# Attention of batches 2 to 7 gathered into four visits per batch of up to seven PSUM banks, with the next batch's projections joined to the last visit

## The chip, the cores and the metric

The kernel runs on one core of a Trainium2 chip. The metric is the device time of one execution in microseconds (us), the median of several runs.

## The reference

Linformer attention, then a feed-forward block with hard-swish, in float32. The kernel's matmuls take bfloat16 operands.

```python
# q, k, v: [8 batches, 8 heads, 1024, 64];  E, F: [64, 1024]
k_proj = einsum('ks,bhsd->bhkd', E, k)
v_proj = einsum('ks,bhsd->bhkd', F, v)
attn = softmax(q @ k_proj^T / 8)                 # over 64 projected positions
x = (attn @ v_proj)  -> [8192 tokens, 512]
# w_in: [512, 2048];  w_out: [2048, 512]
h = x @ w_in
out = (h * clip(h + 3, 0, 6) / 6) @ w_out
```

## The kernel before

Each batch is worked on in two halves `t` of 512 tokens. A half needs 16 **w_in groups** (4 full-array matmuls each, then a Relu on ScalarE and a product on VectorE) and 4 **w_out groups** (16 full-array matmuls each, then a copy and a store). The w_out groups of one half are done between the w_in groups of the next. Attention of batch b+1 is slipped into these groups of batch b, as a generator that is advanced one step after each group.

Attention of one batch has these parts. The matmuls of scores, sums and values use a quarter of the array each (64 rows x 64 columns, a **quadrant**), four side by side, a **round**. Those of the projection use 128 rows x 64 columns, two side by side. Such a way of splitting the array is called a **mode** here:

```python
def project(self):                 # 16 matmuls, each 128 rows x 64 columns of the array, one bank
    ps = self.ps = pat()
    for so in range(SO):
        for e in range(2):
            nc.tensor.matmul(ps[e * KP:(e + 1) * KP], ef_t[e][:, so, :], ...)

def scores(self, j):               # 8 quadrant matmuls, two banks, emptied by two Exp on ScalarE
    ...
def normalised(self, j):           # 8 quadrant matmuls, four banks
    den = self.quads(lambda r, h: ones[r:r + KP, :D], j)      # sums: two banks
    av = self.quads(lambda r, h: self.vp[r:r + KP, h, :], j)  # values: two banks
    lns = [log(den[t]) for t in range(NB)]                    # ScalarE
    yield
    for t in range(NB):                                       # 1/x = exp(-ln x) on ScalarE
        nc.vector.tensor_mul(self.xT[:, j, t, :], av[t], inverse(lns[t]))
        yield
```

The order in time is a plan of (steps to wait, part). Batches are counted from 0, as the code does. Batch 0 is done by a class of its own, batches 1 and 2 have plans of their own, and batches 3 to 7 use this one:

```python
PLAN = ((0, "project"), (1, "keys_out"), (0, "values_out", 0), (0, "values_out", 1), (1, "turn"),
        (6, "two_scores", 0), (3, "normalised", 0), (1, "normalised", 1),
        (1, "two_scores", 2), (3, "normalised", 2), (1, "normalised", 3))
PLANS = {1: (...), 2: (...)}
```

That makes seven places per batch where attention interrupts the stream of full-array matmuls, called **visits** here. PSUM, which the matmuls write to, is split into four banks for the feed-forward (`pmm`, "mm") and four for attention (`pat`, "at"):

```python
ps_mm = ctx.enter_context(tc.tile_pool(name="ps_mm", bufs=4, space=bass.MemoryType.PSUM))
ps_at = ctx.enter_context(tc.tile_pool(name="ps_at", bufs=4, space=bass.MemoryType.PSUM))
```

The softmax here doesn't subtract the row's maximum and nothing guards it: scores larger than these inputs give would overflow.

## Time and profile before

| | before |
|---|---|
| time, median of 4 runs | 518.1 us |
| span of the profiled run | 516.5 us |
| TensorE busy | 502.4 us, 97% |
| ScalarE, VectorE busy | 282.0 us, 239.4 us |
| one batch in the steady part (projection to projection) | 61.24 us |

The profile shows one execution. Its page has busy times by engine and the chain of waits that ended last. Its timeline lists instructions in order of time: start, duration from the first start to the last end, engine, source line, operation, output and inputs, shape, count, and in brackets the idle time ahead and what ended it. The ends of matmuls are modelled, so "busy" overlaps and hides gaps. Starts are what to trust: the steady step from one full matmul to the next is 0.216 us. About one full matmul in forty has no record (2048 are issued and 1998 recorded), so a lone jump of 0.216 us, often printed as "0.16 <-issue", is a lost record and no wait. The lines are shown inside the prediction.

### The profile page before, as it was taken

What the parts mean: (1) busy time and instruction counts of PE and PEld (TensorE: products, weight loads), DVE (VectorE), ACT (ScalarE), POOL (GpSimd) and SP (SyncE); (2) the same over time, 40 slices, a digit from 0 to 9 for tenths busy, and PEclk for the clock granted to TensorE, in tenths of its full rate; (3) what the DMA queues carried; (4) which work ended last, traced back from release to release, by engine and by line L of the source; (5) the groups of instructions that cost most, each with busy time, mean ns of one, the idle gap of its engine ahead of it and who ended that gap; (6) DMA issues with size and microseconds to landing.
All of it is one profiled execution on the core that took longest, in us unless ns stands there. A gap on an engine that the chain in (4) does not pass through costs nothing.

```text
span 516.5 us, 7173 instructions
## 1 busy us (share of the span) xinstructions
PE 502.4 (97%) x2752; PEld 222.7 (43%) x2802; DVE 239.4 (46%) x377; ACT 282.0 (55%) x517; POOL 37.2 (7%) x56
## 2 busy tenths in 40 slices
PE   8899999999999999999999999999999999999996
PEld 4444444434344444444444444444444444444442
DVE  3573735744455345445444453544535544344420
ACT  3657466575556743766436753566545674444431
POOL 8510020020020000200010000200000000000000
PEclk9999999999999999999999999999999999999999
DMA  9999999499169511984119820397111011001112
GB/s 169 202 204 208 202 162 209 93 155 212 41 103 214 123 43 30 153 175 102 41 52 188 175 67 34 70 205 151 41 42 39 34 42 41 28 35 43 41 43 80
DMA packets 73683, 55.40 MB, mean 107 GB/s; under 512 B 35504, under 2 KB 65456, under 8 KB 73648
## 3 DMA queue, kind: packets, MB, share of 16 engines
q0 software_dynamic: 31424, 29.36, 36.0%
q1 hardware_dynamic: 42000, 25.17, 18.3%
q8 instruction: 22, 0.36, 0.3%
q10 hardware_dynamic: 224, 0.39, 0.3%
q14 instruction: 13, 0.11, 0.1%
HBM read 59.24 MB, written 16.78 MB: 147 GB/s over the span
## 4 chain that ended last, share of the span: by engine, by line
PE 89%; DMA 3%; ACT 2%; issue 2%; DVE 2%; POOL 1%; another core or an unknown queue 0%; DVEq 0%; ACTq 0%; POOLq 0%
PE mm L421 41%; PE mm L401 41%; PE at L224 3%; PE at L181 3%; DMA w_in_sb<-in_moe_w_in_dram 2%; PE at L210 1%; DMA k<-in_k_dram 1%; DVE g L407 1%; ACT ln L158 0%; ACT r L406 0%; POOL q L97 0%; ACT aT L215 0%; POOL k L101 0%; DVE xT L235 0%
## 5 line engine op out<-in xcount | busy, mean ns | idle before, releaser
L407 DVE SCALAR_TENSOR_TENSOR g<-r,mm 128x512 bf16<-128x512 f32 x256 | 173.2, 685 | 207.0 <-ACT r L406 206.7
L401 PE MATMUL mm<-xT,w_in_sb 128*128 128x512 bf16 x1001 | 232.5, 379 | 3.4 <-issue 1.7
L421 PE MATMUL mm<-w_out_sb,g 128*128 128x512 bf16 x997 | 229.4, 379 | 1.3 <-issue 0.2
L406 ACT ACTIVATE r<-mm 128x512 f32<-128x512 f32 x256 | 152.2, 602 | 67.3 <-PE mm L401 65.6
L401 PEld LDWEIGHTS <-w_in_sb 128*128 128x128 bf16 x1024 | 97.0, 98 | 125.5 <-issue 12.8
L421 PEld LDWEIGHTS <-g 128*128 128x128 bf16 x1024 | 98.9, 98 | 120.6 <-issue 3.8
L435 ACT COPY o_sb<-mm 128x512 f32<-128x512 f32 x59 | 34.3, 586 | 140.0 <-PE mm L421 134.9
L235 DVE TENSOR_TENSOR xT<-at,rec 128x512 bf16<-128x512 f32 x56 | 38.0, 684 | 24.8 <-ACT rec L163 24.8
L163 ACT ACTIVATE rec<-ln 128x512 f32<-128x512 f32 x60 | 37.5, 637 | 0.0
L158 ACT ACTIVATE ln<-at 128x512 f32<-128x512 f32 x60 | 33.0, 615 | 6.2 <-PE at L224 3.9
L215 ACT ACTIVATE aT<-at 128x512 bf16<-128x512 f32 x56 | 29.0, 610 | 2.0 <-PE at L210 2.0
L199 POOL COPY mark<-kT 1x1 bf16<-1x1 bf16 x5 | 0.9, 177 | 246.6 <-DMA kT<-kp 246.6
L224 PE MATMUL at<-aT,vp 64*64 64x512 bf16 x112 | 12.7, 378 | 1.3 <-ACT ln L158 0.8
L181 PE MATMUL at<-k,e_t 128*64 128x512 bf16 x56 | 13.4, 382 | 0.0
L181 PE MATMUL at<-v,f_t 128*64 128x512 bf16 x56 | 13.4, 382 | 0.0
L224 PE MATMUL at<-aT,ones 64*64 64x512 bf16 x112 | 11.5, 400 | 0.1
L210 PE MATMUL at<-qT,kT 64*64 64x256 bf16 x224 | 9.1, 275 | 1.0 <-DVE vp L190 0.9
L190 DVE CAST vp<-at 64x512 bf16<-64x512 f32 x14 | 9.7, 694 | 0.3
L187 DVE CAST kp<-at 64x512 bf16<-64x512 f32 x14 | 8.9, 676 | 1.1 <-PE at L181 1.1
L181 PEld LDWEIGHTS <-e_t 128*64 128x64 bf16 x56 | 5.6, 109 | 7.3 <-issue 3.0
L84 PE MATMUL mm<-ones 128*128 128x512 bf16 x18 | 7.0, 521 | 1.5 <-DVE ones L77 1.5
L224 PEld LDWEIGHTS <-ones 64*64 64x64 bf16 x112 | 3.2, 103 | 11.9 <-issue 11.9
(57 smaller groups left out, 109.0 us busy)
## 6 DMA issues: line engine op xcount, KB each, us to landing
out_dram<-o_sb SPq DMA_DIRECT2D x63, 256.0 KB, 2.0
k<-in_k_dram POOLq DMA_DIRECT2D x7, 1024.0 KB, 14.7
v<-in_v_dram POOLq DMA_DIRECT2D x7, 1024.0 KB, 20.1
q<-in_q_dram POOLq DMA_DIRECT2D x7, 1024.0 KB, 9.8
w_out_sb<-in_moe_w_out_dram POOLq DMA_DIRECT2D x4, 512.0 KB, 18.0
w_in_sb<-in_moe_w_in_dram POOLq DMA_DIRECT2D x3, 512.0 KB, 12.4
k<-in_k_dram POOLq DMA_DIRECT2D x4, 256.0 KB, 5.5
v<-in_v_dram POOLq DMA_DIRECT2D x4, 256.0 KB, 7.7
```

The lines of the kernel that those rows point to most:

```text
L158: nc.scalar.activation(ln, den, AF.Ln)
L163: nc.scalar.activation(rec, ln, AF.Exp, scale=-1.0)
L181: nc.tensor.matmul(ps[e * KP:(e + 1) * KP], ef_t[e][:, so, :], kqv[self.b]["kv"[e]][:, :, so, :], start=(so == 0), stop=(so == SO - 1))
L210: nc.tensor.matmul(tiles[r][t * KP:(t + 1) * KP, a * HT:(a + 1) * HT], self.kT[r * D:(r + 1) * D, 2 * j + a, :], qT[r * D:(r + 1) * D, j, ...
L215: nc.scalar.activation(self.aT[j][:, r].rearrange("p a n -> p (a n)"), tiles[r], AF.Exp, scale=scale)
L224: nc.tensor.matmul(tiles[t][c:c + D].rearrange("p (r n) -> p r n", r=2), stationary(r, 2 * j + a), self.aT[j][r:r + KP, :, a, :], start=Tr ...
L235: nc.vector.tensor_mul(self.xT[:, j, t, :], av[t], inverse(lns[t]))
L401: nc.tensor.matmul(h_ps, w_in_sb[:, ko, fo * P:(fo + 1) * P], xT[:, ko, t, :], start=(ko == 0), stop=(ko == KO - 1))
L406: nc.scalar.activation(r, h_ps, AF.Relu, bias=0.5, scale=1.0 / 6.0)
L407: nc.vector.scalar_tensor_tensor(g[:, fo, :], r, 1.0, h_ps, op0=ALU.min, op1=ALU.mult)
L421: nc.tensor.matmul(o_ps, g[:, fo, c * P:(c + 1) * P], w_out_sb[:, fo, :], start=(fo == 0), stop=(fo == FO - 1))
L435: (copy or nc.scalar.copy)(o_sb, o_ps)
```

## The change

Its intent is to interrupt the stream of full-array matmuls less often. Attention of batches 2 to 7 becomes four visits, each inside a w_out group (after 8 of its 16 matmuls) or, for the last, behind one. To have banks for this, a visit borrows two or three "mm" banks. The copies of these w_out groups move to VectorE. The projection of batch b+2 follows directly on the last visit of batch b+1. The core of the diff (cuts marked "..."):

```diff
-    for lo, n in ((0, 128), (128, 128), (256, 256), (512, 512), (1024, 512), (1536, 512)):
+    for lo, n in ((0, 128), (128, 128), (256, 256), (512, 256), (768, 256),
+                  (1024, 512), (1536, 512)):
         load_w_in(lo, n)
...
+        def visit(self, n, following, later):
+            if n == 0:
+                last = self.scores(2, pmm)
+                firsts = [self.scores(j, pat) for j in range(2)]
+                for j, tiles in zip((2, 0, 1), (last, *firsts)):
+                    self.exps(j, tiles)
+                return lambda: None
+            if n == 1:
+                den, av = self.sums(0, pmm, pmm), self.values(0, pat, pat)
+                last = self.scores(3, pat)
+                recs = self.inverses(den)
+                self.exps(3, last)
+                return lambda: self.scaled(0, av, recs)
+            if n == 2:
+                den, av = self.sums(1, pmm, pmm), self.values(1, pat, pat)
+                more = self.sums(2, pat, pat)
+                ...
+                return lambda: self.scaled(1, av, recs)
+            early = self.values(2, pmm, pmm)
+            den, av = self.sums(3, pmm, pat), self.values(3, pat, pat)
+            if following:
+                following.project()
+            self.scaled(2, early, self.recs)
+            recs = self.inverses(den)
+            if following:
+                following.keys_out()
+                later += [following.turn] + [lambda a=a: following.values_out(a) for a in range(2)]
+            return lambda: self.scaled(3, av, recs)
...
         def normalised(self, j):
-            ...
-            lns = [log(den[t]) for t in range(NB)]
+            den, av = self.sums(j, pat, pat), self.values(j, pat, pat)
+            recs = self.inverses(den)
             yield
-            for t in range(NB):
-                nc.vector.tensor_mul(self.xT[:, j, t, :], av[t], inverse(lns[t]))
-                yield
+            self.scaled(j, av, recs)
+            yield
+            yield
...                                           # batch 1 keeps seven visits; (3, ...2), (1, ...0) become
+            (1, "two_scores", 0), (2, "two_scores", 2), (2, "normalised", 0),
...                                           # in the loop over w_in groups
+                rows = second_group(*behind[0], fo // SB, nc.vector.tensor_copy)
+                if n < 3:
+                    next(rows)
+                    next(rows)                # 8 of the 16 w_out matmuls
+                    rest = second.visit(n, third, later)
+                    whole(rows)
+                else:
+                    whole(rows)
+                    rest = second.visit(n, third, later)
+                rest()
```

Batch 1's visits are in batch 0's feed-forward. Batch 2's are in the second half of batch 1's, because that is the first place with w_out groups. Those of batches 3 to 7 are in the first half of the batch before.

More of the change, by code (lines that the diff above doesn't have):

```diff
@@ L156, in log @@
     def log(den):
-        ln = att.tile([P, TOK], f32, tag="ln", name="ln")
+        ln = att.tile([P, TOK], f32, tag="rec", name="rec", bufs=4)
         nc.scalar.activation(ln, den, AF.Ln)
@@ L161, in inverse, with __init__ @@
     def inverse(ln):
-        rec = att.tile([P, TOK], f32, tag="rec", name="rec")
-        nc.scalar.activation(rec, ln, AF.Exp, scale=-1.0)
-        return rec
+        nc.scalar.activation(ln, ln, AF.Exp, scale=-1.0)
+        return ln
     class Attention:
-        def __init__(self, b, xT):
-            self.b, self.xT = b, xT
+        def __init__(self, b):
+            self.b = b
             self.kp = att.tile([KP, H, 2, D], bf16, tag="kp", name="kp")
@@ L200, in turn, with scores @@
                 load_kqv(self.b + 1, "qkv" if self.b > 1 else "kvq")
-        def scores(self, j):
+        def scores(self, j, alloc):
             qT = qT_dma[self.b]
-            self.aT[j] = att.tile([P, 2, 2, HT], bf16, tag="aT", name="aT", bufs=KO + 1)
-            tiles = [pat() for _ in range(2)]
+            tiles = [alloc() for _ in range(2)]
             for a in range(2):
@@ L213, in scores, with exps @@
                                          start=True, stop=True)
+            return tiles
+        def exps(self, j, tiles):
+            self.aT[j] = att.tile([P, 2, 2, HT], bf16, tag="aT", name="aT", bufs=KO + 1)
             for r in range(2):
@@ L216, in scores, with quads @@
                                      AF.Exp, scale=scale)
-        def quads(self, stationary, j):
-            tiles = [pat() for _ in range(NB)]
+        def quads(self, stationary, j, allocs):
+            tiles = [alloc() for alloc in allocs]
             for t in range(NB):
@@ L227, in quads, with sums, values, inverses @@
             return tiles
+        def sums(self, j, *allocs):
+            return self.quads(lambda r, h: ones[r:r + KP, :D], j, allocs)
+        def values(self, j, *allocs):
+            return self.quads(lambda r, h: self.vp[r:r + KP, h, :], j, allocs)
+        def inverses(self, den):
+            recs = [log(d) for d in den]
+            for rec in recs:
+                inverse(rec)
+            return recs
+        def scaled(self, j, av, recs):
+            for t in range(NB):
+                nc.vector.tensor_mul(self.xT[:, j, t, :], av[t], recs[t])
@@ new lines, in visit @@
+        def visit(self, n, following, later):
[15 more added lines that the diff above has]
+                recs = self.inverses(den)
+                self.recs = []
+                later += [lambda i=i: self.recs.append(log(more[i])) for i in range(NB)]
+                later += [lambda i=i: inverse(self.recs[i]) for i in range(NB)]
+                return lambda: self.scaled(1, av, recs)
[9 more added lines that the diff above has]
+            return lambda: self.scaled(3, av, recs)
@@ L229, in normalised, with two_scores @@
+        def two_scores(self, j):
+            tiles = [self.scores(i, pat) for i in (j, j + 1)]
+            for i in range(2):
+                self.exps(j + i, tiles[i])
         def normalised(self, j):
-            den = self.quads(lambda r, h: ones[r:r + KP, :D], j)
-            av = self.quads(lambda r, h: self.vp[r:r + KP, h, :], j)
-            lns = [log(den[t]) for t in range(NB)]
+            den, av = self.sums(j, pat, pat), self.values(j, pat, pat)
+            recs = self.inverses(den)
@@ L233, in normalised @@
             yield
-            for t in range(NB):
-                nc.vector.tensor_mul(self.xT[:, j, t, :], av[t], inverse(lns[t]))
-                yield
-        def two_scores(self, j):
-            self.scores(j)
-            self.scores(j + 1)
+            self.scaled(j, av, recs)
+            yield
+            yield
         def steps(self, plan):
@@ L247, in steps @@
                 yield from getattr(self, part)(*args) or ()
-    PLAN = ((0, "project"), (1, "keys_out"), (0, "values_out", 0), (0, "values_out", 1), (1, "turn"),
-            (6, "two_scores", 0), (3, "normalised", 0), (1, "normalised", 1),
-            (1, "two_scores", 2), (3, "normalised", 2), (1, "normalised", 3))
-    PLANS = {1: ((0, "project"), (0, "keys_out"), (1, "turn"), (0, "values_out", 0), (2, "values_out", 1),
-                 (1, "two_scores", 0), (3, "two_scores", 2), (1, "normalised", 0),
-                 (0, "normalised", 1), (0, "normalised", 2), (0, "normalised", 3)),
-             2: ((10, "project"), (0, "keys_out"), (1, "turn"), (2, "values_out", 0), (3, "values_out", 1),
-                 (1, "two_scores", 0), (2, "two_scores", 2), (3, "normalised", 0),
-                 (0, "normalised", 1), (1, "normalised", 2), (0, "normalised", 3))}
+    PLAN = ((0, "project"), (0, "keys_out"), (1, "turn"), (0, "values_out", 0), (2, "values_out", 1),
+            (1, "two_scores", 0), (2, "two_scores", 2), (2, "normalised", 0),
+            (0, "normalised", 1), (0, "normalised", 2), (0, "normalised", 3))
     class First:
@@ L470 @@
             first.queries(1, (0, 1) if fo == FO - 2 else (2, 3))
-    ahead = Attention(1, x_next).steps(PLANS[1])
+    ahead = Attention(1)
+    ahead.xT = x_next
+    ahead = ahead.steps(PLAN)
     rows = [second_group(0, 0, g[0], c) for c in range(SB)]
@@ L492 @@
     xT = x_next
-    behind = []
+    behind, later = [], []
+    second = Attention(2)
     for b in range(1, B):
-        ahead = iter(())
         if b + 1 < B:
-            x_next = x_tile()
-            ahead = Attention(b + 1, x_next).steps(PLANS.get(b + 1, PLAN))
+            x_next = second.xT = x_tile()
+        third = Attention(b + 2) if b + 2 < B else None
+        n = 0
         for t in range(NB):
-            if t == 1 and b + 2 < B:
-                qT_dma[b + 2] = q_transposed(b + 2)
+            if b == 1 and t == 1:
+                qT_dma[3] = q_transposed(3)
             g = g_tile()
@@ L506 @@
                 first_group(xT, t, g, fo)
-                next(ahead, None)
-                if behind and fo % SB == SB - 1:
-                    whole(second_group(*behind[0], fo // SB))
-                    next(ahead, None)
+                if later:
+                    later.pop(0)()
+                if b > 1 and t == 0 and fo == 5 and third:
+                    qT_dma[b + 2] = q_transposed(b + 2)
+                if b == 1 and t == 0 and fo == 10:
+                    second.project()
+                    second.keys_out()
+                    later += [second.turn, *(lambda a=a: second.values_out(a) for a in range(2))]
+                if not behind or fo % SB < SB - 1:
+                    continue
+                if b + 1 == B or n == 4:
+                    whole(second_group(*behind[0], fo // SB))
+                    continue
+                rows = second_group(*behind[0], fo // SB, nc.vector.tensor_copy)
[8 more added lines that the diff above has]
+                rest()
+                n += 1
             behind = [(b, t, g)]
-        whole(ahead)
-        xT = x_next
+        second, xT = third, x_next
     for c in range(SB):
```

## The prediction

It was written before any run of the changed kernel.

> **What bounds the kernel now.** I read the page first: engine shares, then the chain that ended last.
>
> ```profile
> PE 502.4 (97%) x2752; PEld 222.7 (43%) x2802; DVE 239.4 (46%) x377; ACT 282.0 (55%) x517; POOL 37.2 (7%) x56
> ...
> PE 89%; DMA 3%; ACT 2%; issue 2%; DVE 2%; POOL 1%; another core or an unknown queue 0%; DVEq 0%; ACTq 0%; POOLq 0%
> ```
>
> TensorE is on the chain nearly everywhere; VectorE and ScalarE have half their time free. So a saving must come from TensorE's own order: idle stretches, or work that runs slower than its neighbours. The 97% hides both, because matmul ends are modelled. I therefore went to the timeline of TensorE and compared start times (its x counts miss a record now and then, so a lone jump of 0.216 us is a lost record). A steady stretch:
>
> ```profile
> 214.64 1.89 PE L401 MATMUL mm<-xT,w_in_sb 128*128 128x512 bf16 x8
> 216.46 0.41 PE L224 MATMUL at<-aT,ones 64*64 64x512 bf16 x4
> 216.70 0.39 PE L224 MATMUL at<-aT,vp 64*64 64x512 bf16 x4
> 217.02 1.90 PE L401 MATMUL mm<-xT,w_in_sb 128*128 128x512 bf16 x8
> 218.76 3.62 PE L421 MATMUL mm<-w_out_sb,g 128*128 128x512 bf16 x15
> ```
>
> A whole w_out group of 16 lasts 3.45 us elsewhere in that view (242.18 to 245.64), so a full-array matmul takes 0.216. The 16 full ones from 214.64 to 218.76 account for 3.45 of 4.12 us; the attention visit between them costs 0.67. Its work is two rounds of four quadrant matmuls. A 512-column round takes 0.2125 (the projection's pairs follow each other at that step), so 0.425. The other **0.24 us is the price of one visit**, half at each edge: the visit starts 0.31 after the last full matmul, and the next full one starts 0.31 after its last round.
>
> Second, real stalls. Attention of batch 2, in the timeline of 84 to 140 us:
>
> ```profile
> 104.25 0.51 PE L210 MATMUL at<-qT,kT 64*64 64x256 bf16 x9
> 105.64 0.41 PE L210 MATMUL at<-qT,kT 64*64 64x256 bf16 x7 [0.88 <-DVE vp L190]
> 105.98 1.90 PE L401 MATMUL mm<-xT,w_in_sb 128*128 128x512 bf16 x8
> ...
> 130.19 0.40 PE L224 MATMUL at<-aT,vp 64*64 64x512 bf16 x2
> 131.44 0.40 PE L224 MATMUL at<-aT,vp 64*64 64x512 bf16 x2 [0.85 <-ACT ln L158]
> 131.78 1.90 PE L401 MATMUL mm<-xT,w_in_sb 128*128 128x512 bf16 x8
> ```
>
> The visit needs an attention bank that VectorE or ScalarE has not emptied. And one at the start, where w_in arrives late:
>
> ```profile
> 22.80 1.46 PE L401 MATMUL mm<-xT,w_in_sb 128*128 128x512 bf16 x6
> 24.60 1.25 PE L401 MATMUL mm<-xT,w_in_sb 128*128 128x512 bf16 x5 [0.35 <-DMA w_in_sb<-in_moe_w_in_dram]
> ```
>
> **What the Trainium skill says.** "TensorEngine Tiling (Array Packing)", Tiling Modes, Key Properties: "Changing tiling mode (not just tile) drains the TensorE". The trace agrees: 0.09 to 0.10 us over the normal step at every edge between 128x128 and 64x64, and between 128x128 and 128x64. It gives no figure; mine is the trace's. "TensorE: Matmul & The Clock Gate", Part 2, says that back-to-back matmuls hide the array's drain (215.7 ns at 512 columns); the trace has 216. "PSUM — Partial Sum Buffer", Specifications, gives eight banks: four "mm" and four "at" here, so a visit that wants seven must borrow from the feed-forward ring.
>
> **The change, part by part.**
>
> *Fewer visits.* The instruction order of both builds has the same 5606 TensorE rows. Before, each of batches 1 to 7 makes 7 visits (projection, two of scores, four of sums and values): 49. After: batch 1 still 7, batch 2's projection 1, batches 2 to 7 four each: 32. That is 17 fewer, at 0.24 (0.25 for a projection, 0.23 for scores): 4.0 us. But five projections are joined to a 64x64 visit and remain another mode (128x64), so one edge each stays: 5 x 0.12 = 0.6. Net **-3.4 us**, all on the path.
>
> *Stalls of batch 2.* An undisturbed visit lasts 0.56 from first to next full matmul (216.46 to 217.02). Those at 104.25, 123.62 and 129.92 last 1.73, 1.02 and 1.86: 2.9 too many. After, batch 2's visits come in the second half of batch 1, one per 6.9 us plus the visit, with mm banks in reserve, and its projection bank is emptied several groups before. **-2.9 us**.
>
> *Stalls of batch 1.* 73.18 and 83.77 last 1.38 (one lost record taken out) and 1.15: 1.4 too many. The second pair of scores comes one step earlier and both products now follow together, ahead of the output copy; the banks come free 0.6 to 0.9 earlier. **-1.4 us**.
>
> *w_in piece halved.* The pieces land at 22.0 and 24.56, 2.55 us for 512 columns; half of that lands at an estimated 23.3, before its use at 24.1. The next half, about 24.6, is needed at 25.8. **-0.5 us**.
>
> *New work on the other engines: none on the path, but one place.* About 24 output copies move from ScalarE (586 ns) to VectorE (685 ns): VectorE 239 to 256 us, still half idle. I walked a steady batch with steps between queued instructions of 0.48 us (ScalarE) and 0.60 (VectorE). After the visit of three scores, six exponentials hold ScalarE for 3.0 us, and the next Relu waits for none of it, since half a w_out group (1.73) and a w_in group (0.86) lie between. The semaphores in the build show that the group after next takes the bank of the first exponential, not that of the output still being copied. After the visit with the projection VectorE has the copy, two products, two key casts and two products before the first Relu product: done an estimated 3.3 us after the visit, needed at 3.45. Tight, but it fits.
>
> *The place.* Batch 2's last visit ends right where batch 2's own feed-forward begins. Its fourth matmul needs the last product, and VectorE casts the keys first. From before:
>
> ```profile
> 98.24 1.28 DVE L187 CAST kp<-at 64x512 bf16<-64x512 f32 x2 [0.56 <-PE at L181]
> ```
>
> The casts end at 99.52, 1.42 us after the projection's next full matmul (98.10). The first product follows at +0.60, 2.03; the matmul was due at 0.66. **+1.4 us**, once. For later batches a half batch of feed-forward lies between.
>
> Sum: 518.07 - 3.4 - 2.9 - 1.4 - 0.5 + 1.4 = 511.3. I put 0.2 on top for small misses: **511.5 us**, -1.3%.
>
> **Rivals.** (a) *Bank waits move into the big visits.* A seven-bank visit needs nearly all of PSUM; if each of the 24 met 0.2 us of wait, 4.8 us would be lost: 516. Against it: the banks' last readers are done 2 us or more ahead in my walk; for it: the margin of 0.15 after the projection visit. (b) *The loads of batch 4.* They are asked for at the start of batch 2's half and its projection comes at the end of it, some 33 us later; before, v landed 21.5 us after the first of the three was issued (147.3 to 168.8), and qT stood in the queue for 13 us under such loads (113.1 to 126.4), holding output stores. By this there are 5 us in hand; if not, 1 to 4 us once. (c) *The edges are not the cost*: if the 0.24 came from waiting weight loads and grew with the visit, nothing of the 3.4 would be saved: 515. Against: the scores' 16 small matmuls pay 0.23, the projection's 16 large ones 0.25. (d) *VectorE becomes the bound around the visits*: 50% on average speaks against it.
>
> **Range and chances.** If all gains hold and the 1.4 shrinks, 510; if batch 1's gain fails and the big visits lose 0.05 to 0.1 each, 514. Range 510.0 to 514.0. Faster by over 2% needs 507.7, 3.8 us that I see nowhere: 0.03. Slower by over 2% (528.4) would need a stall of half a microsecond at each visit and more: 0.01. Within 2%: 0.96.
>
> **What would show it.** Steady batches one projection to the next (61.24 us, 200.71 to 261.94) should come to about 60.65. Visits of 0.09 at each edge, whatever their length, confirm the price; the joined visit should show a third edge. No stall over 0.2 us between 84 and 135 us, none near 24. One stall of 1.4 us at the fourth w_in matmul of batch 2, released by VectorE's product. It is wrong if idle time before w_in or w_out groups after the visits appears, released by VectorE, or if the first visit of a batch waits for its transposed keys.

## The result

The changed kernel takes **511.89 us** (median of 4 runs, 511.63 to 512.01) against 518.1 us (518.07 to 518.32) before. The ratio is 0.9879, with a 95% interval from 0.9861 to 0.9896: faster by 1.2%, within 2%. (A ratio here is the mean time of one kernel's fast runs over that of the other's of the same rounds, so it isn't quite the ratio of the medians quoted.)

The page of the changed kernel, engine shares and chain:

```profile
PE 497.4 (98%) x2750; PEld 224.3 (44%) x2802; DVE 257.5 (50%) x401; ACT 274.5 (54%) x493; POOL 37.9 (7%) x57
...
PE 94%; DMA 3%; issue 1%; POOL 1%; DVE 0%; ACT 0%; DVEq 0%; POOLq 0%
```

ScalarE and VectorE, 2% each of the chain before, are at 0% now (rounded), which fits: by its waits from 20 us on, TensorE stands still for another compute engine once, at the new stall shown below. VectorE has 18 us more to do, ScalarE 7.5 us less, and neither is near its limit.

A joined visit of the steady part, in the timeline of TensorE:

```profile
226.32 0.41 PE L227 MATMUL mm<-aT,vp 64*64 64x512 bf16 x4
226.56 0.38 PE L227 MATMUL mm<-aT,ones 64*64 64x512 bf16 x2
226.57 0.38 PE L227 MATMUL at<-aT,ones 64*64 64x512 bf16 x2
226.78 0.39 PE L227 MATMUL at<-aT,vp 64*64 64x512 bf16 x4
227.09 0.40 PE L181 MATMUL at<-k,e_t 128*64 128x512 bf16 x1
...
228.63 0.38 PE L181 MATMUL at<-v,f_t 128*64 128x512 bf16 x1
228.94 3.41 PE L450 MATMUL mm<-xT,w_in_sb 128*128 128x512 bf16 x15
232.41 3.62 PE L470 MATMUL mm<-w_out_sb,g 128*128 128x512 bf16 x16
```

The step between starts is 0.21 to 0.24 within a mode. It is 0.31 from the quadrants to the projection (226.78 to 227.09) and again from the projection to the full array (228.63 to 228.94): the joined visit has three edges, not four. From 228.94 to 232.41 is 3.47 us, the plain duration of 16 matmuls, so the w_out group after it waits for nothing. One steady batch (projection to projection) is 60.62 us now, from 61.24.

Batch 2's visits, in the same view:

```profile
106.21 0.41 PE L209 MATMUL mm<-qT,kT 64*64 64x256 bf16 x8
106.45 0.61 PE L209 MATMUL at<-qT,kT 64*64 64x256 bf16 x16
106.99 1.90 PE L470 MATMUL mm<-w_out_sb,g 128*128 128x512 bf16 x7
...
121.78 0.41 PE L227 MATMUL mm<-aT,ones 64*64 64x512 bf16 x4
122.02 0.39 PE L227 MATMUL at<-aT,vp 64*64 64x512 bf16 x4
122.24 0.39 PE L227 MATMUL at<-aT,ones 64*64 64x512 bf16 x4
122.56 1.90 PE L470 MATMUL mm<-w_out_sb,g 128*128 128x512 bf16 x8
```

Six banks are filled in 0.78 us each time without an idle mark. The waits of 0.9 us that batch 2's visits had are gone.

And the new stall. TensorE first, then VectorE, in the timeline around batch 2's last visit:

```profile
133.92 0.82 PE L450 MATMUL mm<-xT,w_in_sb 128*128 128x512 bf16 x2
135.98 2.97 PE L450 MATMUL mm<-xT,w_in_sb 128*128 128x512 bf16 x13 [1.25 <-DVE xT L246]
```

```profile
134.05 1.28 DVE L187 CAST kp<-at 64x512 bf16<-64x512 f32 x2 [0.76 <-PE at L181]
135.26 1.27 DVE L246 TENSOR_TENSOR xT<-at,rec 128x512 bf16<-128x512 f32 x2
```

The fourth w_in matmul needs the first of the two products, and VectorE does both key casts ahead of it. By starts the matmul came 1.41 us late.

### The profile page after: what moved, and what is told of

Same layout as the page of the kernel before. It is cut to its first block, busy times and chain, and to the rows that moved or that the text cites. A ratio compares the mean times of both kernels' runs of the same rounds, so it can differ in the third digit from the quotient of the medians.

```text
span 510.0 us, 7106 instructions
## 1 busy us (share of the span) xinstructions
PE 497.4 (98%) x2750; PEld 224.3 (44%) x2802; DVE 257.5 (50%) x401; ACT 274.5 (54%) x493; POOL 37.9 (7%) x57
## 4 chain that ended last, share of the span: by engine, by line
PE 94%; DMA 3%; issue 1%; POOL 1%; DVE 0%; ACT 0%; DVEq 0%; POOLq 0%
PE mm L470 43%; PE mm L450 43%; PE at L181 3%; DMA w_in_sb<-in_moe_w_in_dram 2%; PE at L227 1%; PE mm L227 1%; DMA k<-in_k_dram 1%; PE at L209 1%; PE mm L209 0%; PE at L370 0%; POOL q L97 0%; DVE kp L187 0%; POOL k L101 0%; PE at L350 0%; DVE xT L246 0%
## 5 line engine op out<-in xcount | busy, mean ns | idle before, releaser
L450 PE MATMUL mm<-xT,w_in_sb 128*128 128x512 bf16 x1001 | 229.2, 379 | 3.1 <-DVE xT L246 1.2
L484 ACT COPY o_sb<-mm 128x512 f32<-128x512 f32 x35 | 20.3, 587 | 91.5 <-PE mm L470 91.5
L484 DVE COPY o_sb<-mm 128x512 f32<-128x512 f32 x28 | 19.3, 691 | 67.3 <-PE mm L470 64.2
L159 ACT ACTIVATE rec<-mm 128x512 f32<-128x512 f32 x34 | 19.0, 595 | 34.1 <-PE mm L227 17.6
L163 ACT ACTIVATE rec<-rec 128x512 f32<-128x512 f32 x60 | 35.6, 637 | 0.0
L246 DVE TENSOR_TENSOR xT<-at,rec 128x512 bf16<-128x512 f32 x44 | 28.1, 680 | 7.1 <-ACT rec L163 7.1
L218 ACT ACTIVATE aT<-at 128x512 bf16<-128x512 f32 x44 | 23.1, 613 | 0.9 <-PE at L209 0.9
L159 ACT ACTIVATE rec<-at 128x512 f32<-128x512 f32 x30 | 17.3, 598 | 6.0 <-PE at L227 3.7
L218 ACT ACTIVATE aT<-mm 128x512 bf16<-128x512 f32 x12 | 6.5, 594 | 8.9 <-PE mm L209 8.9
L227 PE MATMUL at<-aT,vp 64*64 64x512 bf16 x88 | 8.5, 376 | 0.0
```

The costliest lines, as they stand in the source:

```text
L159: nc.scalar.activation(ln, den, AF.Ln)
L163: nc.scalar.activation(ln, ln, AF.Exp, scale=-1.0)
L218: nc.scalar.activation(self.aT[j][:, r].rearrange("p a n -> p (a n)"), tiles[r], AF.Exp, scale=scale)
L227: nc.tensor.matmul(tiles[t][c:c + D].rearrange("p (r n) -> p r n", r=2), stationary(r, 2 * j + a), self.aT[j][r:r + KP, :, a, :], start=Tr ...
L246: nc.vector.tensor_mul(self.xT[:, j, t, :], av[t], recs[t])
L450: nc.tensor.matmul(h_ps, w_in_sb[:, ko, fo * P:(fo + 1) * P], xT[:, ko, t, :], start=(ko == 0), stop=(ko == KO - 1))
```

## The experiments

Eleven runs; all results were correct. "Now" is the changed kernel, 511.89 us. Each experiment was timed beside the kernel before. Differences of a few tenths between whole times are not read as effects of an edit: the changed kernel itself took 511.89 and 511.42 us, and its first w_in matmul started at 20.68 us in one profile, where it waited 0.73 us for its weights to land, and at 20.36 in the other (19.9 to 21.0 over all runs).

### Is it the change of the array's mode that costs? Four runs

Theory: each change between ways of splitting the array costs about 0.12 us, whatever lies between. Rivals: any interruption costs it; or attention's own data and waits do; or it grows with the visit; or joining a projection is free. The last batch has no attention, so extra visits of a known kind can be put there: one after each of its 32 w_in groups, with matmuls of ones into an attention bank that nothing reads.

```diff
                 first_group(xT, t, g, fo)
+                if b + 1 == B:
+                    extra()
...
+    def extra():                                  # d_full
+        ps = pat()
+        for _ in range(2):
+            nc.tensor.matmul(ps, ones[:, :P], ones, start=True, stop=True)
+    def extra():                                  # d_quad; d_long has range(4)
+        ps = [pat(), pat()]
+        for _ in range(2):
+            for r in range(2):
+                for c in range(2):
+                    nc.tensor.matmul(ps[r][c * D:(c + 1) * D], ones[r * D:(r + 1) * D, :D],
+                                     ones[r * D:(r + 1) * D], start=True, stop=True)
+                                                  # d_mixed: range(1), then
+        for c in range(2):
+            nc.tensor.matmul(ps[0][c * D:(c + 1) * D], ones[:, :D], ones, start=True, stop=True)
```

> Changed kernel with 32 extra interruptions in the last batch (which has no attention), one after each w_in group: two full-array 128x512 matmuls of ones into a free attention bank, never read; the result stays right. Theory (the price is for changing the array's mode, not for interrupting): 32 x 2 x 0.216 = +13.8 us on 511.9, so 525.7. Rival (any interruption of the stream costs 0.24): 533.4.

> The same 32 places with two rounds of four 64x64 quadrant matmuls instead, the same array time. Theory: 32 x (0.425 + 0.24) = +21.3 us, so 533.2, that is 7.5 us over the full-array twin. Rival (the 0.24 comes from attention's own weights, data or waits, which the extra visits do not have): 525.5.

> The same 32 places with four rounds of quadrant matmuls. Theory (a price per visit): 32 x (0.85 + 0.24) = +34.9 us, so 546.8. Rival (the price grows with the rounds, 0.12 each): 32 x (0.85 + 0.48), so 554.5.

> The same 32 places with one round of quadrant matmuls and then one pair of 128x64 matmuls. Theory (each edge between modes costs 0.12, three edges here): 32 x (0.425 + 0.36) = +25.1 us, so 537.0. Rival (only leaving and re-entering the full mode costs, a joined projection is free): 533.2.

| run | time, us | ratio to before | edges per visit | per visit, by whole times |
|---|---|---|---|---|
| d_full | 525.32 | 1.0141 | 0 | +0.42 over now; its own two matmuls take 0.43 |
| d_quad | 532.39 | 1.0277 | 2 | +0.22 over d_full (7.07 / 32) |
| d_long | 546.60 | 1.0553 | 2 | +0.44 over d_quad (14.21 / 32), its two more rounds take 0.43 |
| d_mixed | 536.48 | 1.0356 | 3 | +0.13 over d_quad (4.09 / 32) |

One visit in the timeline of TensorE, first d_full, then d_quad, then d_mixed:

```profile
455.73 0.59 PE L550 MATMUL at<-ones 128*128 128x512 bf16 x2
456.16 1.03 PE L450 MATMUL mm<-xT,w_in_sb 128*128 128x512 bf16 x4
457.02 0.59 PE L550 MATMUL at<-ones 128*128 128x512 bf16 x2
```

```profile
459.18 0.63 PE L552 MATMUL at<-ones 64*64 64x512 bf16 x8
459.74 1.04 PE L450 MATMUL mm<-xT,w_in_sb 128*128 128x512 bf16 x4
460.71 0.63 PE L552 MATMUL at<-ones 64*64 64x512 bf16 x8
```

```profile
458.83 0.41 PE L552 MATMUL at<-ones 64*64 64x512 bf16 x4
459.17 0.41 PE L555 MATMUL at<-ones 128*64 128x512 bf16 x2
459.51 1.04 PE L450 MATMUL mm<-xT,w_in_sb 128*128 128x512 bf16 x4
460.48 0.41 PE L552 MATMUL at<-ones 64*64 64x512 bf16 x4
```

In d_full two matmuls and four come round in 1.29 us, which is 6 x 0.216 and nothing else. In d_quad the same array time takes 1.53, so 0.24 more. In d_mixed it takes 1.65. All four rivals fall: an interruption in the full mode is free, ones that wait for nothing pay the same as attention does, doubling the visit doesn't raise the price, and a change from 64x64 to 128x64 is charged like any other. Since d_long also has twice as many small matmuls and weight loads per visit as d_quad, their number is not what costs.

The whole times of the table also carry the scatter of the start. From the end of batch 7's projection to the last matmul, by starts, it is 155.64 us now, 169.45 in d_full, 176.83 in d_quad, 190.64 in d_long and 180.69 in d_mixed. Per visit that is 0.43 for two full matmuls, **0.23 for the two edges**, 0.43 for two more rounds and **0.12 for the third edge**, close to the single lines.

What fills the time at an edge is not shown. Within a mode the trace has each weight load start one matmul ahead of its use. At an edge it starts with its own matmul (both at 216.46 in the kernel before, 0.31 after the last full one), and a load lasts about 0.10 us. An array that has to empty first and a load that cannot go ahead would look the same here.

### Is it the number of visits in the changed kernel?

```diff
             if n == 0:
                 last = self.scores(2, pmm)
-                firsts = [self.scores(j, pat) for j in range(2)]
+                next(rows)                        # four more w_out matmuls
+                firsts = [self.scores(0, pat)]
+                next(rows)
+                firsts.append(self.scores(1, pat))
...
                 den, av = self.sums(0, pmm, pmm), self.values(0, pat, pat)
+                next(rows)
                 last = self.scores(3, pat)
...                                           # in the loop: the first visit starts after 4 matmuls, not 8
                     next(rows)
-                    next(rows)
-                    rest = second.visit(n, third, later)
+                    if n > 0:
+                        next(rows)
+                    rest = second.visit(n, third, later, rows)
```

> Changed kernel with the first visit of each of batches 2 to 7 cut into three and the second into two, each piece four w_out matmuls after the one before: 18 more visits, nothing else. Theory: 18 x 0.235 = +4.2 us on 511.9, so 516.1. Rival (the gain came from bank waits removed, not from fewer visits): 511.9.

Measured: 515.84 us (ratio to before 0.9953), 3.95 us over now, 0.22 for each of the 18 visits added. A steady batch goes from 60.62 to 61.31 us, 0.23 for each of three. The first visit, now in three pieces, in the timeline of TensorE:

```profile
201.73 0.41 PE L209 MATMUL mm<-qT,kT 64*64 64x256 bf16 x8
202.30 0.81 PE L474 MATMUL mm<-w_out_sb,g 128*128 128x512 bf16 x3 [0.16 <-issue]
203.04 0.41 PE L209 MATMUL at<-qT,kT 64*64 64x256 bf16 x8
203.39 1.04 PE L474 MATMUL mm<-w_out_sb,g 128*128 128x512 bf16 x4
204.35 0.41 PE L209 MATMUL at<-qT,kT 64*64 64x256 bf16 x8
```

From 203.04 to 204.35 is 1.31 us: four full matmuls (0.86), two rounds of 256 columns (0.22) and 0.23 of edges. (The row with three matmuls has lost one record.) The same work in more pieces costs what the pieces' edges cost.

### Batch 1's order of steps and the halved w_in piece alone

```diff
# kernel before
-        (256, 256), (512, 512), (1024, 512), (1536, 512)
+        (256, 256), (512, 256), (768, 256), (1024, 512), (1536, 512)
...                       # batch 1 alone; "joined" is the changed kernel's normalised()
-                 (1, "two_scores", 0), (3, "two_scores", 2), (1, "normalised", 0),
-                 (0, "normalised", 1), (0, "normalised", 2), (0, "normalised", 3)),
+                 (1, "two_scores", 0), (2, "two_scores", 2), (2, "joined", 0),
+                 (0, "joined", 1), (0, "joined", 2), (0, "joined", 3)),
```

> Kernel before with the halved w_in piece and batch 1's new order of steps (second scores one step earlier, both products together) and nothing else. Theory: 1.4 us of bank waits at two visits of batch 1 and 0.5 us of the wait near 24 us go: 518.1 - 1.9 = 516.2. Rival (these waits return further on, in the loads or the transposes of batch 1): 518.

Measured: 516.36 us, 1.79 under its kernel before (518.15; ratio 0.9966). From batch 1's projection to batch 2's, the profile has 39.61 us instead of 41.03: 1.42 less. The timeline of TensorE at the start and at the last of batch 1's visits:

```profile
21.83 4.52 PE L412 MATMUL mm<-xT,w_in_sb 128*128 128x512 bf16 x20
...
83.01 0.41 PE L224 MATMUL at<-aT,ones 64*64 64x512 bf16 x4
83.25 0.39 PE L224 MATMUL at<-aT,vp 64*64 64x512 bf16 x4
83.57 1.90 PE L432 MATMUL mm<-w_out_sb,g 128*128 128x512 bf16 x8
```

The 20 matmuls run through the place at 24 us where the stream had broken off for w_in. The visit lasts 0.56 instead of 1.15. From the first w_in matmul to batch 1's projection it is 35.87 us instead of 36.39, 0.52 less; in this profile that first matmul came 0.58 later than before, which hides the gain at the projection itself. Neither wait comes back later.

### Batch 2's waits alone

```diff
# kernel before, batch 2 alone, visits where they were
-             2: ((10, "project"), (0, "keys_out"), (1, "turn"), (2, "values_out", 0), (3, "values_out", 1),
-                 (1, "two_scores", 0), (2, "two_scores", 2), (3, "normalised", 0),
-                 (0, "normalised", 1), (1, "normalised", 2), (0, "normalised", 3))}
+             2: ((10, "project"), (0, "keys_out"), (1, "turn"), (0, "values_out", 0), (1, "values_out", 1),
+                 (5, "two_scores", 0), (2, "two_scores", 2), (3, "joined", 0),
+                 (0, "joined", 1), (1, "joined", 2), (0, "joined", 3))}
```

> Kernel before with only batch 2's steps changed, visits as before: its values are cast out of the projection bank three and five steps earlier, the reciprocals follow their logarithms at once and both products come together. Theory (waits for undrained attention banks cost 2.9 us at three visits of batch 2): 518.1 - 2.9 = 515.2, with undisturbed visits of 0.56 us. Rival (they waited for the batch's loads and transposed queries, which the change only moved out of the way): 517.5 to 518.5.

Measured: 516.24 us, 1.92 under its kernel before (518.16; ratio 0.9965). From batch 2's projection to batch 3's it is 39.82 us instead of 41.67, 1.86 less. The rival falls, but 1.0 to 1.1 us of the 2.9 is still there. (By the plan the values are cast two and four steps earlier, not three and five.) In the timeline of TensorE, then of VectorE:

```profile
103.34 1.02 PE L412 MATMUL mm<-xT,w_in_sb 128*128 128x512 bf16 x4 [0.20 <-DVE g L418]
...
122.59 0.41 PE L224 MATMUL at<-aT,ones 64*64 64x512 bf16 x4
123.05 0.40 PE L224 MATMUL at<-aT,vp 64*64 64x512 bf16 x2
123.65 0.40 PE L224 MATMUL at<-aT,vp 64*64 64x512 bf16 x2 [0.19 <-DVE xT L245]
123.98 3.63 PE L432 MATMUL mm<-w_out_sb,g 128*128 128x512 bf16 x16
```

```profile
121.71 0.69 DVE L418 SCALAR_TENSOR_TENSOR g<-r,mm 128x512 bf16<-128x512 f32 x1 [3.36 <-ACT r L417]
122.31 1.28 DVE L245 TENSOR_TENSOR xT<-at,rec 128x512 bf16<-128x512 f32 x2
```

The early casts themselves held up a w_in group, at 103.34, by 0.14 us by starts (a record is lost just before it). The visit at 106.69 takes 0.66, so 0.10 too much. And the visit at 122.59 takes 1.39 instead of 0.56, more than the 1.02 it took in the kernel before. That makes 1.07 us, all that is left.

The visit at 122.59 waits for the products of the visit before it, which lies only 3.45 us of w_in groups back. ScalarE first does a copy, two logarithms and two reciprocals (118.58 to 121.19) and then the first Relu (to 121.68). The two products stand in VectorE's queue behind the w_in product that needs this Relu. They end at 123.00 and 123.60, and the two pairs of matmuls start 0.05 later each. So with visits this close the new order made the wait longer. In the changed kernel a w_in run and a whole w_out group's worth of matmuls (6.9 us) lie between visits, and this visit's wait is gone. That the spacing took it away is read from the traces; no run changed the spacing alone.

### Does the copy's move to VectorE matter?

```diff
-                rows = second_group(*behind[0], fo // SB, nc.vector.tensor_copy)
+                rows = second_group(*behind[0], fo // SB)          # copy on ScalarE
```

> Changed kernel with the output copies of the visits' w_out groups back on ScalarE. Theory (VectorE and ScalarE have slack around the visits and the bank of the copy is reused last): 511.9 within 0.4. Rival (ScalarE's queue of exponentials delays the copy and with it a bank): 1 to 3 us slower, by up to 0.1 us at each of 24 visits.

Measured: 512.05 us (ratio to before 0.9883), 0.16 over now and within the scatter, with a steady batch of 60.62 us and the stall before batch 2's fourth w_in matmul unchanged (34.40 us from batch 3's projection to batch 4's in both). The move neither helps nor hurts.

### Taking the new stall away

```diff
             recs = self.inverses(den)
+            self.scaled(3, av, recs, (0,))        # the first half's product, ahead of the key casts
             if following:
                 following.keys_out()
                 ...
-            return lambda: self.scaled(3, av, recs)
+            return lambda: self.scaled(3, av, recs, (1,))
```

> Changed kernel with one VectorE instruction moved: in the last visit the first product of the last head pair goes ahead of the two key casts. Theory: the 1.4 us stall of the fourth w_in matmul of batch 2 vanishes, 511.9 - 1.4 = 510.5, and the keys of batch 3 come an estimated 0.2 us later, still before their first use. Rival (that matmul is also held by ScalarE's reciprocal, or the keys then come late): 511.5 to 512.

Measured: 510.39 us (ratio to before 0.9849). VectorE and TensorE in the timeline of this run:

```profile
133.70 0.69 DVE L246 TENSOR_TENSOR xT<-at,rec 128x512 bf16<-128x512 f32 x1 [0.30 <-ACT rec L163]
134.31 1.27 DVE L187 CAST kp<-at 64x512 bf16<-64x512 f32 x2
```

```profile
134.02 3.63 PE L451 MATMUL mm<-xT,w_in_sb 128*128 128x512 bf16 x15
137.49 1.89 PE L471 MATMUL mm<-w_out_sb,g 128*128 128x512 bf16 x8
```

The product starts while TensorE is still on the projection, and the w_in stream is unbroken (134.02 to 137.49 is 16 x 0.216 and 0.01). The key casts start 0.29 us after the first full matmul instead of 0.13, and the keys' transpose landed at 138.25, ahead of the scores at 139.31.

Both kernels were run once more on one other chip:

> The changed kernel once more, on the chip of the other run, so that these can be compared with it: 511.9.

> The best version once more beside the changed kernel: 510.4, so 1.5 us under it, if the earlier difference was not the chip's. If it was: equal.

The changed kernel: 511.42 us (ratio to before 0.9871). With the product first: **509.96 us** (0.9843). The difference is 1.46 us, as before. This is the version that beats both: 1.6% under the kernel before.

## Why the prediction was right

The prediction was 511.5 us; 511.89 and, on a second chip, 511.42 were measured. Step by step:

- **What bounds it: right.** Every gain came from TensorE's stream, and the busy times of ScalarE and VectorE, which moved by 7.5 and 18 us, didn't matter.
- **Fewer visits, -3.4 us: right.** 17 visits at the 0.23 of d_quad and of split_visits' steady batches are 3.9; five edges at the 0.12 of d_mixed take 0.6 back. That is 3.3 us. The steady batch was foretold at about 60.65 and came to 60.62.
- **Stalls of batch 2, -2.9: right in sum, and 1.9 of it shown by itself.** The cause named, undrained banks, holds; the spacing of the visits turned out to be part of it. The changed kernel has one delay of 0.14 us left by starts, in a w_in group at 102.66 us. Its trace shows why: batch 2's second value cast held VectorE until 101.89, so the product that empties the group's bank ended at 102.61. That is the same delay as in batch2_order.
- **Stalls of batch 1 and the w_in piece, -1.4 and -0.5: right.** head_only has 1.42 and 0.52 less in the two stretches, 1.8 in time. The changed kernel has the same 35.87 and 39.61 us there in both its profiles.
- **The new stall, +1.4: right,** at the matmul named and released by VectorE's product: 1.41 us by starts, and 1.46 to 1.5 when it was taken away. One slip: the matmul needs the first of the last pair's two products, not "the last product"; the prediction's sum uses the first.
- **The rivals.** The big visits wait for no bank: the waits of TensorE in the changed kernel from 20 us on are one on VectorE and one on the first w_in piece, beside marks of lost records. Batch 4's v landed at 161.9 for a projection at 166.5, so 4.6 us were left of the 5 estimated. The edges are the cost. VectorE is not the bound.

Summed from the runs, the gain is 0.5 + 1.4 + 3.3 + 2.8 - 1.4 = 6.6 us. From the first w_in matmul to the end the profiles have 496.1 us before and 489.4 in both profiles of the changed kernel: 6.8 less (the terms leave 0.2 of it open), which is the prediction's own sum before it added 0.2 for small misses. The rest of the difference in time is the start of that first matmul (20.37 us before, 20.68 and 20.36 after), which the prediction didn't treat. So the 0.2 stood for no miss that the runs show, and how near 511.5 came is in part luck.

## What to carry to other kernels

When TensorE is the bound and reads 97% busy, compare the starts of its matmuls: the price of a change between full-array and tiled matmuls, and waits for undrained banks, are inside the busy share. Put tiled work together so that the mode changes seldom, borrowing idle banks for it, and leave more stream between two visits than the other engines need to empty what the first one filled. Where a joined visit ends just before its own result is needed, put the instruction that makes that result ahead of anything whose use is later.

## What the Trainium skill lacked or had wrong

- "TensorEngine Tiling (Array Packing)", Tiling Modes, says that a change of tiling mode drains the engine, without a size. Here: 0.09 to 0.10 us over the step at an edge in the trace and some 0.02 more at the step after it; 0.23 us per visit of two edges, and no more for a visit twice as long; 0.12 us for an edge between 64x64 and 128x64.
- "TensorE: Matmul & The Clock Gate", Back-to-back issue gap, gives 131 ns per matmul of 512 columns as the sustained rate of weight loads and matmuls in a real kernel. Here the step of the full-array stream is 216 ns, with a new weight load for each matmul, which is what the section gives for isolated ones (and Part 2 of the page, as the prediction quotes it, for back-to-back ones).
- No page on reading profiles tells that matmul records can be missing: 1998 of 2048 full matmuls are in the trace before, and the gap that a lost one leaves is printed as a short idle time.
